# The fourth token tile of a fused SSM and SwiGLU kernel: transposed by DMA, and multiplied after six feature tiles

## The chip, the cores and the metric

The kernel runs on one core of a Trainium2 chip, in one launch. The metric is the device time in microseconds. A core has five engines with queues of their own: TensorE (PE; its weight loads are PEld), VectorE (DVE), ScalarE (ACT), GpSimd (POOL) and SyncE (SP), which here only issues DMAs. Matmul results land in PSUM, eight banks of 128 partitions by 512 fp32 values, and DVE or ACT moves them to SBUF.

## What is computed

2048 tokens of 512 features are layer-normalised; the result goes through a diagonal complex state space model (SSM) and through a SwiGLU feed-forward block, and both are added to the input:

```python
xn = layernorm(x)                                 # x: [1, 2048, 512], bf16
# SSM, 512 complex states
Lam_bar = exp(exp(log_dt) * Lambda)
B_bar = ((Lam_bar - 1) / Lambda)[:, None] * B
h[t] = Lam_bar * h[t - 1] + B_bar @ xn[t]
a = 2 * real(C @ h) + xn * Dskip
# feed-forward, 1376 hidden features
f = (silu(xn @ w_gate) * (xn @ w_up)) @ w_down
out = x + a + f
```

## The kernel before, in words

The tokens are cut into 16 tiles of 128 and four chunks of 512. The hidden features are cut into 11 feature tiles, ten of 128 and one of 96. All matmuls on normalised tokens read xnT, which holds them transposed: [128, 4 pieces k of the model width, 2048 tokens].

For a chunk, `gateup_tile` makes one feature tile: 4 matmuls (L441, one for each k) over 512 tokens into a bank for the gate, 4 into another for the up projection. `gu_out` then has ACT apply Silu to the first (L455, into guT) and copy the second (L456, into u), and for every second feature tile a product of two tiles (L460, on DVE) is put into the list `products`. `bproj_tile` (L366, evicted at L368) is the input projection of the SSM: four tiles with the real part of B, four with the imaginary part. Their weights are BT, the transposed B, which eight DMA transposes from DRAM (L140) fill. The rotations (L376 to L390, with sine and cosine tables s16 and c16), scans (L408) and rotations back of the SSM run on DVE. After that come the down projection (L575, L549) and the output of the SSM (L587), whose operand CF is made on ACT (L349) and DVE (L352).

**The first chunk** starts before all its tokens are there. Its four token tiles arrive one by one: `ln_stats` (L197, L198), the reciprocal root (L202), `norm_dve` (L214, in place in xall), then `xT_pe`: four TensorE transposes (L231) into two banks and two copies (L238, L240) into xnT. Feature tiles 0 to 2 hold six banks (`held`); `head_mm` (L676) adds the tokens that have come, 128 or 256 columns at a time. Token tile 3 is the last: `norm_dve(3)` at L713, `xT_pe(3)` at L716, and at L726 to L730 each of feature tiles 0 to 2 gets its last 128 columns and is evicted. Feature tiles 3 to 6 follow over the whole 512 columns (L785), and then the eight `bproj_tile`s of chunk 0 (L789), feature tiles 7 to 10 (L804), and `bproj_chunk(1)` (L812). The token tiles of chunks 1 to 3 are transposed by DMA: `xT_dma` (L245), which SP issues when the tile has been normalised (chunk 1 by DVE, L214; chunks 2 and 3 by ACT, L219, which needs nb of L209, which needs L205 and GpSimd's L206). The function `up_halves` (L485) is the first to read chunk 3.

**The order of the work** is the order of the program on each engine; nothing is reordered. SP's queue at the start is written out at L121 to L146: x, the weights in four groups of feature tiles (0 and 1; 2; 3 to 6; 7 to 9), x of chunk 1, four transposes of the real part of B, the last weight group, four transposes of the imaginary part, and w_last.

Work of DVE and ACT that isn't tied to a matmul (`table_ops`, the layer norm of later chunks, the SSM) stands in a backlog, each piece with a cost in us written by hand. `pump(us)` adds to a balance, and emits pieces from the backlog while the balance is at least half the cost of the next; each piece takes its cost off. `multiply(keep)` emits products until `keep` are left and takes 0.65 off for each. GU is 1.73, the cost of a feature tile; BP is 0.87. So the place of such a piece in the queue of its engine, between two evictions say, depends on how much has been pumped. `need(tag)` emits all that a tag still has.

Of the kernel before, what the change touches and what calls it, by code (L numbers as in the profile page):

```python
# [11 lines left out]
BF16 = mybir.dt.bfloat16  # L12
ALU = mybir.AluOpType
ACT = mybir.ActivationFunctionType
# [9 lines left out]
def kernel(  # L24
# [17 lines left out]
    nc = tc.nc  # L42
    _, L, D = A_x.shape
    Pst = A_Lambda_re.shape[0]
    F = B_w_gate.shape[1]
    assert L % 512 == 0 and D % 128 == 0 and Pst % 128 == 0 and Pst == D
    CW = 512
# [3 lines left out]
    TPC = CW // 128  # L51
    KD = D // 128
    NQ = Pst // 128
    FT = (F + 127) // 128
    fsz = [min(128, F - i * 128) for i in range(FT)]
# [3 lines left out]
    LA, LB = 32, 64  # L59
    FL = (FT - 1) * 128  # L60
# [6 lines left out]
    up_p = ctx.enter_context(tc.tile_pool(name="up_p", bufs=4))  # L67
# [5 lines left out]
    def bank(shape=(128, CW), dtype=F32):  # L73
        return psum.tile(list(shape), dtype, name="ps")
# [4 lines left out]
    x_v = A_x[0].rearrange("(n p) d -> p n d", p=128)  # L79
    out_v = out[0].rearrange("(n p) d -> p n d", p=128)  # L80
    wg_v = B_w_gate.rearrange("(k p) f -> p k f", p=128)
    wu_v = B_w_up.rearrange("(k p) f -> p k f", p=128)


    xall = const.tile([128, NT, D], BF16, name="xall")
    xnT = const.tile([128, KD, L], BF16, name="xnT")

    fgroups = [(0, 2), (2, 3), (3, 7), (7, FT - 1)]
    wg_g, wu_g = [], []
# [4 lines left out]
    w_last = const.tile([128, KD, 128], BF16, name="w_last")  # L94
    wu_last = const.tile([128, KD, LB], BF16, name="wu_last")
    wd_sb = const.tile([128, FT - 1, D], BF16, name="wd_sb")
    BT = const.tile([128, 2, KD, Pst], BF16, name="BT")
# [6 lines left out]
    def wslice(groups, fi, k):  # L104
        for (a, b), t in zip(fgroups, groups):
            if a <= fi < b:
                return t[:, k, (fi - a) * 128:(fi - a) * 128 + fsz[fi]]


    def load_w1(q, tiles, view, gi):  # L110
        a, b = fgroups[gi]
        q.dma_start(out=tiles[gi][:], in_=view[:, :, a * 128:min(F, b * 128)])
# [20 lines left out]
        nc.gpsimd.dma_start(out=prm_rows[i * NQ:(i + 1) * NQ, :], in_=v.rearrange("(q j) -> q j", j=128))  # L133
    load_w1(nc.sync, wg_g, wg_v, 2)
    load_w1(nc.sync, wu_g, wu_v, 2)
    for n in (TPC, TPC + 2):
        nc.sync.dma_start(out=xall[:, n:n + 2, :], in_=x_v[:, n:n + 2, :])
    for part, src in enumerate((A_B_re, A_B_im)):
        for k in range(KD):
            nc.sync.dma_start_transpose(out=BT[:, part, k, :], in_=src[:, k * 128:(k + 1) * 128])  # L140
        if part == 0:
            load_w1(nc.sync, wg_g, wg_v, 3)
            load_w1(nc.sync, wu_g, wu_v, 3)

    nc.sync.dma_start(out=w_last[:, :, 0:LB + LA], in_=wg_v[:, :, FL:F])
    nc.sync.dma_start(out=w_last[:, :, LB + LA:128], in_=wu_v[:, :, FL + LB:F])  # L146

    def load_late():
        nc.sync.dma_start(out=wu_last[:], in_=wu_v[:, :, FL:FL + LB])
# [43 lines left out]
    def xn_tile(c):  # L193
        return xn_end if c == NCH - 1 else xall[:, c * TPC:(c + 1) * TPC, :]
# [17 lines left out]
    def norm_dve(n, lo=0, hi=D):  # L212
        c, i = divmod(n, TPC)
        nc.vector.tensor_scalar(out=xn_tile(c)[:, i, lo:hi], in0=xall[:, n, lo:hi], scalar1=mv[:, n, 0:1],  # L214
                                scalar2=rstd[:, n:n + 1], op0=ALU.subtract, op1=ALU.mult)
# [8 lines left out]
    def xT_pe(n, on_dve=(), prm_too=False):  # L224

        c, i = divmod(n, TPC)
        for h in range(2):
            tp = bank((128, HK * 128 + 128), BF16)
            for k in range(HK):
                lo = (h * HK + k) * 128  # L230
                nc.tensor.transpose(out=tp[:, k * 128:(k + 1) * 128], in_=xn_tile(c)[:, i, lo:lo + 128],  # L231
                                    identity=ident[:])
            if prm_too and h == 1:
                prm_transpose(tp[:, HK * 128:])
            dst = xnT[:, h * HK:(h + 1) * HK, n * 128:(n + 1) * 128]
            src = tp[:, 0:HK * 128].rearrange("p (k t) -> p k t", k=HK)
            if h in on_dve:
                nc.vector.tensor_copy(out=dst, in_=src)  # L238
            else:
                nc.scalar.copy(out=dst, in_=src)  # L240
        return tp[:, HK * 128:]

    def xT_dma(n):
        c, i = divmod(n, TPC)
        nc.sync.dma_start_transpose(out=xnT[:, :, n * 128:(n + 1) * 128], in_=xn_tile(c)[:, i, :])  # L245
# [12 lines left out]
    V = nc.vector  # L258

    def prm_transpose(pp):  # L260
        nc.tensor.transpose(out=pp, in_=prm_rows[:], identity=ident[:])
# [173 lines left out]
    u_pair = {}  # L435
    products = []

    def gu_mm(ps, groups, c, fi, lo, hi):
        fs = fsz[fi]
        for k in range(KD):  # L440
            nc.tensor.matmul(ps[:fs, lo:hi], lhsT=wslice(groups, fi, k),  # L441
                             rhs=xnT[:, k, c * CW + lo:c * CW + hi], start=(k == 0), stop=(k == KD - 1))

    def gu_tile(c):
        if c not in gu_tiles:
            gu_tiles[c] = gut.tile([128, FT - 1, CW], BF16, name="guT")
        return gu_tiles[c]

    def gu_out(c, fi, psg, psu):

        guT = gu_tile(c)
        fs = fsz[fi]
        if fi % 2 == 0:
            u_pair[c] = up_p.tile([128, 2, CW], BF16, name="u2")
        nc.scalar.activation(out=guT[:fs, fi, :], in_=psg[:fs], func=ACT.Silu)  # L455
        nc.scalar.copy(out=u_pair[c][:fs, fi % 2, :], in_=psu[:fs])  # L456
        if fi % 2 == 1:
            lo = fi - fi % 2
            g, u = guT[:fs, lo:fi + 1, :], u_pair[c][:fs, 0:fi - lo + 1, :]
            products.append(lambda: V.tensor_tensor(out=g, in0=g, in1=u, op=ALU.mult))  # L460

    up_last = {}

# [40 lines left out]
    def gateup_tile(c, fi):  # L504
        if fi == FT - 1:
            return gateup_last(c)
        psg = bank()
        gu_mm(psg, wg_g, c, fi, 0, CW)
        psu = bank()
        gu_mm(psu, wu_g, c, fi, 0, CW)  # L510
        gu_out(c, fi, psg, psu)
# [97 lines left out]
    def queue(tag, ops, at=None):  # L609
        ops = [[op[0], op[1], op[2] if len(op) > 2 else None, tag] for op in ops]  # L610
        if at is None:
            backlog.extend(ops)
        else:
            backlog[at:at] = ops

    def step():
        for item in backlog[0:AHEAD + 1]:
            if item[2] is not None:
                item[2]()
                item[2] = None  # L620
        cost, op, _, _ = backlog.pop(0)
        op()
        owed[0] -= cost

    def pump(us):

        owed[0] += us
        while backlog and owed[0] >= backlog[0][0] * 0.5:
            step()
        if not backlog:  # L630
            owed[0] = 0.0

    def multiply(keep):

        while len(products) > keep:
            products.pop(0)()
            owed[0] -= 0.65
# [7 lines left out]
    GU = 8 * 0.2163  # L645
    BP = 4 * 0.2163
    H = 3
    held = [(bank(), bank()) for _ in range(H)]
# [23 lines left out]
    def head_mm(which, lo, hi, ks, fis):  # L672

        for fi in fis:
            for k in ks:
                nc.tensor.matmul(held[fi][which][:, lo * 128:hi * 128], lhsT=wslice((wg_g, wu_g)[which], fi, k),  # L676
                                 rhs=xnT[:, k, lo * 128:hi * 128], start=(k == 0), stop=(k == KD - 1))

    allk = range(KD)
# [31 lines left out]
    params_a(pp)  # L711
    head_mm(1, 0, 2, allk, (2,))
    norm_dve(3)  # L713
    head_mm(0, 2, 3, range(0, HK), range(H))
    head_mm(1, 2, 3, range(0, HK), range(H))
    xT_pe(3, on_dve=(0, 1))  # L716
    head_mm(0, 2, 3, range(HK, KD), range(H))
    head_mm(1, 2, 3, range(HK, KD), range(H))
    tables = table_ops()
# [3 lines left out]
    queue("tables", tables[2:3])  # L723
    queue("ln1", norm1)
    queue("tables", tables[3:4] + [(0.1, params_sin)] + tables[4:])
    for fi in range(H):  # L726
        head_mm(0, 3, 4, allk, (fi,))
        head_mm(1, 3, 4, allk, (fi,))
        gu_out(0, fi, *held[fi])
        pump(GU / 4)  # L730
    pump(2.0)

    def bproj_chunk(c):
        need(f"ln{c}")
# [47 lines left out]
        queue(f"ssm{c}", fwd + back)  # L782

    G0 = 7
    for fi in range(H, G0):  # L785
        gateup_tile(0, fi)
        pump(GU)
        multiply(1)
# [72 lines left out]
```

## Time and profile before

| what | value |
|---|---|
| median of 3 runs | 178.78 us (178.36 to 178.89) |
| the profiled execution | 178.79 us |
| its span, first to last instruction | 177.0 us |
| granted TensorE clock | 1.000 |
| busy: PE, DVE, ACT, POOL | 173.4, 154.0, 94.2, 51.3 us |
| matmuls at L441 over 512 columns | 296 |
| DMA transposes on SP: L140, L245 | 8 of 1.18 to 1.36 us, 12 of 1.19 to 1.25 us |
| their time from issue to landing, min/median/max | 3.0/4.5/6.5 us at L140, 2.4/2.4/3.1 us at L245 |

The timeline gives start and length of instructions in us from the span's start, merged where neighbours are alike; what stands in brackets is the idle time of the engine before the instruction and what ended it. SPq is SP's queue: its rows are the issues of DMAs, not the transfers. The DMA view has the time from issue to landing. A matmul row that stands alone shows its whole latency, so costs of TensorE are read from the starts of neighbours, or from the pieces of the chain of work that ended last, which don't overlap.

### The profile page before, as it was taken

What the parts mean: (1) busy time and instruction counts of PE and PEld (TensorE: products, weight loads), DVE (VectorE), ACT (ScalarE), POOL (GpSimd) and SP (SyncE); (2) the same over time, 40 slices, a digit from 0 to 9 for tenths busy, and PEclk for the clock granted to TensorE, in tenths of its full rate; (3) what the DMA queues carried; (4) which work ended last, traced back from release to release, by engine and by line L of the source; (5) the groups of instructions that cost most, each with busy time, mean ns of one, the idle gap of its engine ahead of it and who ended that gap; (6) DMA issues with size and microseconds to landing.
All of it is one profiled execution on the core that took longest, in us unless ns stands there. A gap on an engine that the chain in (4) does not pass through costs nothing.

```text
span 177.0 us, 2543 instructions
## 1 busy us (share of the span) xinstructions
PE 173.4 (98%) x927; PEld 82.3 (46%) x927; DVE 154.0 (87%) x234; ACT 94.2 (53%) x167; POOL 51.3 (29%) x85
## 2 busy tenths in 40 slices
PE   8999999999999999999999999999999999999993
PEld 2984444444444444444444444444444444444443
DVE  3789997999999996899999999999999999993033
ACT  3468898967299649923766661053866610001300
POOL 6050300000300050003999640058185250001410
PEclk9999999999999999999999999999999999999999
DMA  5998745996141016900000020019659600000662
GB/s 169 279 297 215 141 88 122 361 206 111 22 88 31 4 28 117 348 11 2 20 17 19 15 67 24 4 17 132 88 78 178 116 9 0 0 0 6 63 99 74
DMA packets 30764, 16.23 MB, mean 92 GB/s; under 512 B 19680, under 2 KB 30560, under 8 KB 30720
## 3 DMA queue, kind: packets, MB, share of 16 engines
q1 hardware_dynamic: 24704, 11.44, 27.9%
q0 software_dynamic: 5184, 4.07, 16.0%
q10 hardware_dynamic: 864, 0.56, 1.0%
q8 instruction: 7, 0.11, 0.3%
q14 instruction: 5, 0.04, 0.1%
HBM read 8.33 MB, written 5.24 MB: 77 GB/s over the span
## 4 chain that ended last, share of the span: by engine, by line
PE 96%; DMA 1%; DVE 1%; issue 0%
PE ps L441 36%; PE ps L587 16%; PE ps L366 16%; PE ps L575 10%; PE ps L549 10%; PE ps L676 3%; PE ps L496 2%; PE ps L538 2%; DMA xall<-in_A_x_dram 1%; PE ps L485 1%; PE ps L231 1%; DVE stats L197 0%; PE ps L653 0%; DVE xall L214 0%; DVE stats L684 0%; DVE res L592 0%
## 5 line engine op out<-in xcount | busy, mean ns | idle before, releaser
L441 PE MATMUL ps<-xnT,wu 128*128 128x512 bf16 x148 | 38.0, 379 | 0.0
L441 PE MATMUL ps<-xnT,wg 128*128 128x512 bf16 x148 | 38.0, 379 | 0.0
L408 DVE TENSOR_TENSOR_SCAN g<-r_t,car,u 128x512 bf16<-128x512 f32 x24 | 28.7, 1260 | 0.0
L455 ACT ACTIVATE guT<-ps 128x512 bf16<-128x512 f32 x40 | 24.4, 611 | 7.3 <-PE ps L441 5.5
L366 PE MATMUL ps<-xnT,BT 128*128 128x512 bf16 x128 | 28.3, 379 | 0.0
L587 PE MATMUL ps<-CF,wt 128*128 128x512 bf16 (+2 forms) x144 | 28.2, 356 | 0.0
L456 ACT CAST u<-ps 128x512 bf16<-128x512 f32 x40 | 23.9, 598 | 5.6 <-PE ps L441 5.6
L600 ACT CAST res<-ps 128x512 bf16<-128x512 f32 x12 | 6.7, 590 | 36.0 <-PE ps L587 26.8
L181 POOL DMA_DIRECT2D gu_rows<-ul x36 | 17.6, 498 | 18.1 <-DVE ul L473 18.1
L441 PEld LDWEIGHTS <-wu 128*128 128x128 bf16 x148 | 14.5, 98 | 17.4
L441 PEld LDWEIGHTS <-wg 128*128 128x128 bf16 x148 | 14.4, 98 | 17.2
L368 ACT CAST u<-ps 128x512 bf16<-128x512 f32 x32 | 18.4, 591 | 5.1 <-PE ps L366 4.9
L601 POOL DMA_DIRECT2D out_dram<-res x12 | 10.6, 1224 | 34.3 <-ACT res L600 34.2
L587 PEld LDWEIGHTS <-wt 128*128 128x128 bf16 x144 | 13.3, 98 | 15.0 <-issue 0.8
L366 PEld LDWEIGHTS <-BT 128*128 128x128 bf16 x128 | 12.5, 98 | 15.1
L206 POOL TENSOR_TENSOR rstd<-ve,neg_half 128x4 f32<-128x4 f32 x3 | 5.2, 1730 | 47.0 <-DVE ve L205 47.0
L575 PE MATMUL ps<-wd_sb,guT 128*128 128x512 bf16 x80 | 17.6, 379 | 0.0
L549 PE MATMUL ps<-wd_sb,guT 128*128 128x512 bf16 x80 | 17.4, 379 | 0.0
L460 DVE TENSOR_TENSOR guT<-guT,u 128x1024 bf16<-128x1024 bf16 x20 | 13.5, 678 | 0.0
L575 PEld LDWEIGHTS <-guT 128*128 128x128 bf16 x80 | 7.8, 98 | 9.4
L549 PEld LDWEIGHTS <-guT 128*128 128x128 bf16 x80 | 7.8, 98 | 9.5
L197 DVE BATCH_NORM_STATS2 stats<-xall 128x6 f32<-128x512 bf16 x14 | 9.5, 677 | 1.9 <-DMA xall<-in_A_x_dram 1.9
(114 smaller groups left out, 194.7 us busy)
## 6 DMA issues: line engine op xcount, KB each, us to landing
out_dram<-in_A_x_dram SPq DMA_DIRECT2D x1, 1536.0 KB, 7.1
out_dram<-res POOLq DMA_DIRECT2D x12, 128.0 KB, 3.5
out_dram<-xall POOLq DMA_DIRECT2D x3, 512.0 KB, 7.6
wd_sb<-in_B_w_down_dram SPq DMA_DIRECT2D x2, 640.0 KB, 9.0
xall<-in_A_x_dram SPq DMA_DIRECT2D x1, 1024.0 KB, 7.2
gu_rows<-ul POOLq DMA_DIRECT2D x36, 8.0 KB, 1.6
wg<-in_B_w_gate_dram SPq DMA_DIRECT2D x1, 512.0 KB, 5.0
wu<-in_B_w_up_dram SPq DMA_DIRECT2D x1, 512.0 KB, 6.1
```

What stands on the lines that cost most here:

```text
L181: nc.gpsimd.dma_start(out=gu_rows[c][i * RT:(i + 1) * RT, p, :], in_=product[p * RT:(p + 1) * RT, i * 128:(i + 1) * 128])
L366: nc.tensor.matmul(ps[:], lhsT=BT[:, part, k, q * 128:(q + 1) * 128], rhs=xnT[:, k, c * CW:(c + 1) * CW], start=(k == 0), stop=(k == KD - 1))
L368: nc.scalar.copy(out=u_tiles[c][:, part, q, :], in_=ps[:])
L408: V.tensor_tensor_scan(out=g()[:, part, q, :], data0=r_t[:, q:q + 1].to_broadcast([128, CW]), data1=u_tiles[c][:, part, q, :], initial=ini ...
L441: nc.tensor.matmul(ps[:fs, lo:hi], lhsT=wslice(groups, fi, k), rhs=xnT[:, k, c * CW + lo:c * CW + hi], start=(k == 0), stop=(k == KD - 1))
L455: nc.scalar.activation(out=guT[:fs, fi, :], in_=psg[:fs], func=ACT.Silu)
L456: nc.scalar.copy(out=u_pair[c][:fs, fi % 2, :], in_=psu[:fs])
L460: products.append(lambda: V.tensor_tensor(out=g, in0=g, in1=u, op=ALU.mult))
L549: nc.tensor.matmul(o[:], lhsT=gu_tiles[k][:, fi, i * 128:(i + 1) * 128], rhs=wd_sb[:, fi, :], start=(fi == 0), stop=False)
L575: nc.tensor.matmul(o[:], lhsT=gu_tiles[c][:, fi, i * 128:(i + 1) * 128], rhs=wd_sb[:, fi, lo:hi], start=(fi == 0), stop=False)
L587: nc.tensor.matmul(o, lhsT=w_tiles[c][:, part, q, i * 128:(i + 1) * 128], rhs=CF[:, part, q, lo:hi], start=(fresh and part == 0 and q == 0 ...
L601: nc.gpsimd.dma_start(out=out_v[:, n, :], in_=res[:], accum_op=ALU.add)
```

## The change

Token tile 3 of chunk 0 is no longer transposed by TensorE. After `norm_dve(3)`, SP issues `xT_dma(3)`, and the loads that stood behind chunk 1's x in SP's queue now follow it, in a function `load_mid`: both parts of B first, then the last weight group and w_last. The two loads of chunk 1's x become one.

Feature tiles 0 to 2 are evicted over the first 384 columns (EC) as soon as token tile 2 is in. Feature tiles 3 to 5 are then made over the same 384 columns, first the three gates, then the three ups. Token tile 3 comes after that, for six feature tiles: `end_mm` puts 128 columns of four gates into one bank and of four ups into another, then two gates and two ups into a third; `end_out` evicts them, four tiles' gates at once and two tiles' ups at once. The products of pairs 0 and 1, 2 and 3, 4 and 5 are listed only then. The pumps have other sizes. From feature tile 6 on the program is as before. The lines ahead are those of the kernel before.

```diff
     load_w1(nc.sync, wu_g, wu_v, 2)
-    for n in (TPC, TPC + 2):
-        nc.sync.dma_start(out=xall[:, n:n + 2, :], in_=x_v[:, n:n + 2, :])
-    for part, src in enumerate((A_B_re, A_B_im)):
-        for k in range(KD):
-            nc.sync.dma_start_transpose(out=BT[:, part, k, :], in_=src[:, k * 128:(k + 1) * 128])
-        if part == 0:
-            load_w1(nc.sync, wg_g, wg_v, 3)
-            load_w1(nc.sync, wu_g, wu_v, 3)
-
-    nc.sync.dma_start(out=w_last[:, :, 0:LB + LA], in_=wg_v[:, :, FL:F])
-    nc.sync.dma_start(out=w_last[:, :, LB + LA:128], in_=wu_v[:, :, FL + LB:F])
+    nc.sync.dma_start(out=xall[:, TPC:2 * TPC, :], in_=x_v[:, TPC:2 * TPC, :])
+
+    def load_mid():
+        for part, src in enumerate((A_B_re, A_B_im)):
+            for k in range(KD):
+                nc.sync.dma_start_transpose(out=BT[:, part, k, :], in_=src[:, k * 128:(k + 1) * 128])
+        load_w1(nc.sync, wg_g, wg_v, 3)
+        load_w1(nc.sync, wu_g, wu_v, 3)
+        nc.sync.dma_start(out=w_last[:, :, 0:LB + LA], in_=wg_v[:, :, FL:F])
+        nc.sync.dma_start(out=w_last[:, :, LB + LA:128], in_=wu_v[:, :, FL + LB:F])
...
-    def gu_out(c, fi, psg, psu):
...
+    def product(c, fi):
+        g, u = gu_tile(c)[:, fi - 1:fi + 1, :], u_tile(c, fi)[:]
+        products.append(lambda: V.tensor_tensor(out=g, in0=g, in1=u, op=ALU.mult))
+
+    def gu_out(c, fi, psg, psu, hi=CW):
+
+        nc.scalar.activation(out=gu_tile(c)[:, fi, 0:hi], in_=psg[:, 0:hi], func=ACT.Silu)
+        nc.scalar.copy(out=u_tile(c, fi)[:, fi % 2, 0:hi], in_=psu[:, 0:hi])
+        if fi % 2 == 1 and hi == CW:
+            product(c, fi)
...
     norm_dve(3)
+    xT_dma(3)
+    load_mid()
     head_mm(0, 2, 3, range(0, HK), range(H))
     head_mm(1, 2, 3, range(0, HK), range(H))
-    xT_pe(3, on_dve=(0, 1))
     head_mm(0, 2, 3, range(HK, KD), range(H))
     head_mm(1, 2, 3, range(HK, KD), range(H))
...
+    EARLY = 2 * H
+    EC = (TPC - 1) * 128
     for fi in range(H):
-        head_mm(0, 3, 4, allk, (fi,))
-        head_mm(1, 3, 4, allk, (fi,))
-        gu_out(0, fi, *held[fi])
-        pump(GU / 4)
-    pump(2.0)
+        gu_out(0, fi, *held[fi], hi=EC)
+    psg = [bank() for fi in range(H, EARLY)]
+    for fi in range(H, EARLY):
+        gu_mm(psg[fi - H], wg_g, 0, fi, 0, EC)
+        pump(GU * 3 / 8)
+    for fi in range(H, EARLY):
+        psu = bank()
+        gu_mm(psu, wu_g, 0, fi, 0, EC)
+        gu_out(0, fi, psg[fi - H], psu, hi=EC)
+        pump(GU * 3 / 8)
+
+    def end_mm(ps, at, groups, fi):
+        for k in range(KD):
+            nc.tensor.matmul(ps[:, at * 128:(at + 1) * 128], lhsT=wslice(groups, fi, k), rhs=xnT[:, k, EC:CW],
+                             start=(k == 0), stop=(k == KD - 1))
+
+    def end_out(fis, psg, psu):
+        guT = gu_tile(0)
+        nc.scalar.activation(out=guT[:, fis[0]:fis[-1] + 1, EC:CW],
+                             in_=psg.rearrange("p (f t) -> p f t", t=128), func=ACT.Silu)
+        for i in range(0, len(fis), 2):
+            nc.scalar.copy(out=u_tile(0, fis[i])[:, :, EC:CW],
+                           in_=psu[:, i * 128:(i + 2) * 128].rearrange("p (f t) -> p f t", t=128))
+            product(0, fis[i + 1])
+
+    psg, psu = bank(), bank()
+    for ps, groups in ((psg, wg_g), (psu, wu_g)):
+        for fi in range(4):
+            end_mm(ps, fi, groups, fi)
+    end_out(range(4), psg[:], psu[:])
+    pump(GU)
+    multiply(1)
+    ps = bank()
+    for i, groups in enumerate((wg_g, wu_g)):
+        for fi in range(4, EARLY):
+            end_mm(ps, 2 * i + fi - 4, groups, fi)
+    end_out(range(4, EARLY), ps[:, 0:256], ps[:, 256:512])
+    pump(GU / 2)
+    multiply(1)
...
-    for fi in range(H, G0):
+    for fi in range(EARLY, G0):
         gateup_tile(0, fi)
```

More of the change, by code (lines that the diff above doesn't have):

```diff
@@ L447, in gu_tile, with u_tile @@
         return gu_tiles[c]
-    def gu_out(c, fi, psg, psu):
[L451 to L460, printed above, removed]
+    def u_tile(c, fi):
+        if (c, fi // 2) not in u_pair:
+            u_pair[c, fi // 2] = up_p.tile([128, 2, CW], BF16, name="u2")
+        return u_pair[c, fi // 2]
+    def product(c, fi):
[6 more added lines that the diff above has]
+            product(c, fi)
     up_last = {}
```

## The prediction

> **What bounds it now.** I read the chain of work that ended last first, because it says which engine to price: 96% of the span is TensorE, and its pieces join without a hole through the head.
>
> ```profile
> 9.86 0.22 PE ps L231 x4
> 10.09 2.01 PE ps L676 x36
> 12.10 6.91 PE ps L441 x32
> 19.00 6.91 PE ps L366 x32
> 25.91 5.18 PE ps L441 x24
> ```
>
> The reader is to see that each piece starts where the last ended, and the unit prices: 0.22/4 = 55 ns for a transpose, 2.01/36 = 55.8 ns for a matmul over 128 columns with its own weight load, 6.91/32 = 215.9 ns for one over 512. So the kernel can gain only what leaves TensorE, and it loses every wait that TensorE is given; nothing later gives it back, since the chain is TensorE to the end.
>
> Next I read the timeline of SP, whose queue the change reorders.
>
> ```profile
> 7.03 5.37 SPq L140 DMA_TRANSPOSE BT<-in_A_B_re_dram  x4
> 12.45 0.58 SPq L112 DMA_DIRECT2D wg<-in_B_w_gate_dram  x1
> 13.08 1.14 SPq L112 DMA_DIRECT2D wu<-in_B_w_up_dram  x1
> 14.26 5.09 SPq L140 DMA_TRANSPOSE BT<-in_A_B_im_dram  x4
> 19.41 0.58 SPq L145 DMA_DIRECT2D w_last<-in_B_w_gate_dram  x1
> 20.03 0.51 SPq L146 DMA_DIRECT2D w_last<-in_B_w_up_dram  x1
> 22.03 5.16 SPq L245 DMA_TRANSPOSE xnT<-xall  x4
> ```
>
> SP issues one thing after another and a transpose holds it 1.3 us. Last, DVE, ACT and TensorE where the change shifts their order: three places where one waits for another.
>
> ```profile
> 9.11 0.40 DVE L214 TENSOR_SCALAR xall<-xall,mv,rstd 128x512 bf16<-128x512 bf16 x1
> ...
> 30.34 1.23 DVE L376 TENSOR_TENSOR pm<-u,c 128x2048 bf16<-128x2048 bf16 x1 [1.12 <-ACT c L305]
> ...
> 61.78 0.16 DVE L205 TENSOR_SCALAR ve<-mv 128x4 f32<-128x4 f32 x1
> 61.90 1.22 DVE L386 TENSOR_TENSOR wt<-pm 128x2048 bf16<-128x2048 bf16 x1
> 63.04 0.68 DVE L460 TENSOR_TENSOR guT<-guT,u 128x1024 bf16<-128x1024 bf16 x1
> 64.03 0.16 DVE L209 SCALAR_TENSOR_TENSOR nb<-mv,rstd 128x4 f32<-128x4 f32 x1 [0.30 <-POOL rstd L206]
> ```
>
> ```profile
> 64.22 0.81 ACT L219 ACTIVATE xn_end<-xall,nb,rstd 128x512 bf16<-128x512 bf16 x1 [3.16 <-DVE nb L209]
> ```
>
> ```profile
> 72.46 1.92 PE L485 MATMUL ps<-xnT,wu_last 128*64 128x512 bf16 x16
> ```
>
> The reader is to see that DVE at 30.34 waits for a sine on ACT, and that the transposed chunk 3, which L485 reads, hangs on DVE's L209 through ACT's L219.
>
> **TensorE's own work.** Four transposes go: 4 x 55 = 0.220 us. The 24 matmuls of feature tiles 3 to 5 over 512 columns become 24 over 384 and 24 over 128; tile 3 of features 0 to 2 keeps its 24. A 384-wide one isn't in the trace; on the line between 55.8 and 215.9 ns it is 162.5, so a pair costs 2.4 ns more, 0.06 us for 24 (bounds: nothing, and 24 x 55.8 = 1.34 us if a pair cost a whole extra narrow one; the rows lie on the line, so I take 0.06). Net: **-0.16 us**. The 0.06 comes from 128-wide matmuls at 55.8 ns each. The Trainium skill (TensorE: Matmul & The Clock Gate, Back-to-back issue gap) speaks against the split: it gives about 81 ns for a 128-wide and 131 ns for a 512-wide matmul when weight loads alternate with matmuls, by which, as an estimate on its line, each split would cost 64 ns and the net would be +1.2 us. The trace disagrees, 36 such in 2.01 us, so this gets no part of the sum.
>
> **Token tile 3 by DMA.** Its normalisation (L214) ends at 9.52 and moves by nothing: everything ahead of it on DVE and TensorE stays. In 22.03's row the issue follows its normalisation by 0.03, so SP issues at 9.55. Landing is 2.4 us after issue where SP's queue is otherwise idle (median of L245), and 5.9 for the first L140 of 7.03, which stood behind 1.5 MB of loads; so 11.95 to 15.4. That row itself landed at 12.9 and only needed those loads drained, so I take 12.9. It is read after feature tiles 3 to 5: tile 2 ends at 10.76 - 0.22 = 10.54, then 24 x 162.5 ns = 3.90, so 14.44. Hidden by 1.5 us. The weights of feature tile 3 are now read at 10.54 and not 11.9; they landed at 4.26 + 5.0 = 9.3, the up half at 10.9 against 12.5.
>
> **The moved loads.** SP now has nothing from 6.0 to 9.55, and all of L140, the last weight group and w_last stand behind the wait for that normalisation. Issues: 9.55 tile 3, then spacing 1.30 (5.16 for four at L245, its first gap 1.32): B_re from 10.87 to 14.77, B_im from 16.07 to 19.97 (before: 14.26 to 18.10). B_re lands 3.0 later, 17.8, and is read from 18.7: hidden. The last B_im landed 3.0 after issue, the last row of L140; its neighbours of C_im took 2.6 to 3.8. So it lands at 22.97 (22.6 to 23.9). L366 starts at 18.84 and the matmul with the fourth k of B_im is its 20th: 18.84 + 19 x 0.2159 - 0.16 = 22.78, its weight load 0.1 earlier. TensorE waits about **0.3 us** (0 to 1.2), where before it had 1.6 to spare. (L366 began before B_im had landed, so a matmul doesn't wait for all of BT; if it waits for a whole part, it is 0.9 us.) Gate group 3 is issued at 21.3 and read at 25.7: with 4.6 us to landing, as at 12.45, it would be 0.2 late, but then B_re stood in front with 1.35 us between their landings, so 24.4. Chunk 1's four transposes end SP's line by 29.4 + 2.4 = 31.8 at worst, 30.6 with short issues; they are read at 31.6. In SP's file that has a us or none; I take none.
>
> The price of the transposes that decides here is SP's 1.3 us. The Trainium skill (DMA: Bandwidth & Descriptors, Latency and other measured facts) gives DMA transposes 261 GB/s, an estimated 0.5 us for 128 KB; by that B_im would have landed by 18 and the 0.3 us were nothing. The rows have 1.30 between issues with the DMA engines half idle (share 0.46 from 18.84 to 25.75), so the row goes into the sum.
>
> **ACT and banks.** 5 more instructions, and the first six evictions start near 10.1 instead of 11.02. Back to back they are 0.48 us apart at 512 columns, 0.37 at 384; TensorE fills a bank each 0.65. Two banks are free at 10.54 (tile 2's, copied by 9.2), the third is held[0]'s, read by 10.6. No wait; nothing, unless ACT lags by more than the 1.2 us until the third is wanted.
>
> **The ledger of queued work.** This is the second place that can cost. Up to feature tile 6 the pumps were 3 x 0.43 + 2.0 + 3 x 1.73 = 8.49 us, less two products at 0.65; now 6 x 0.65 + 1.73 + 0.87 = 6.49, less the same. All queued work is 2.0 us of cost later in the program, about one feature tile. DVE is in time at first (two copies of 0.28 gone), its second half c ends at 29.3 as before. But the sine behind it is now emitted after feature tile 8, not 7: that copy starts at 29.24, the sine 0.5 later, so L376 starts at 30.84, **0.5 late**, and DVE has no hole until L205. Two products of chunk 1 (0.6 each) are now ahead of L205: 61.78 + 0.5 + 1.2 = 63.5. L205 to L209 takes 2.25 (61.78 to 64.03), to ACT 0.19: 65.9. In the rows the four L219 reach from 64.22 to 68.06; now one more copy (0.47) stands among them, so the last starts at 70.2, ends at 71.0, lands by 73.5. L485 reads chunk 3 from its ninth matmul on, 72.46 + 9 x 0.116 - 0.16 = 73.3. TensorE waits **0.2 us** (0 to 0.9), where it had 2.0 to spare. Chunk 2's, by the same steps, land at 56.3 and are read at 56.7.
>
> **Sum.** -0.16 + 0.3 + 0.2 = +0.34 us on the profiled execution's 178.79 (span 177.0 and 1.8 around it), which is the median of the runs, 178.78. I predict **179.1 us**. A measurement of this kernel can tell about 0.3%, 0.54 us, from no change.
>
> **The rivals.**
> A, all hidden: B_im lands 2.6 after issue and chunk 3 in time: -0.16, 178.6. For it: C_im's shortest landing. Against: SP's four extra us ahead of L140.
> B, slower: SP's queue is what decides. From the point where the fourth B_im lands after 22.7, each further us is a us. With 3.8 to landing (C_im's longest) and 1.36 between issues (B_re's, 5.37 for four) it lands at 24.2: 1.5 us of wait, 180.3. For it: loads may still share the DMA engines; against: those are drained by then.
> C, slower: the ledger is dearer than I price it, and chunk 3 or the CF operands behind it are 0.8 us late: with 0.3 for B_im, 179.7.
> D, tile 3's transpose lands at 15.4 (5.9 after issue) and the change only moves the wait: 1.0 us in place of 0.22: 180.1 with the rest.
> E, faster by more than 0.54: TensorE would have to hold idle time that its rows don't show.
>
> **How the numbers follow.** Forecast (both waits small, -0.1 to +0.54) 0.43, A 0.10, B 0.27, C 0.12, D 0.05, E 0.03. Within 0.3%: 0.43 + 0.10 = 0.53; slower: 0.44; faster: 0.03. The range reaches from A (178.5) past B (180.5).
>
> **What would show it.** In the profile after: SP's L245 at 9.55 ahead of both L140; no L231 at 9.8; 24 pairs at L441 in 3.9 us. Right: a hole of TensorE near 22.7 waiting for a DMA into BT, and one near 73.4 at L485; L376 starts near 30.8. Wrong: no hole at 22.7 (then SP or landing is faster than the rows), a hole near 14.4 (D), or one where I have none, such as at 25.7 or 31.6.

## The result and the profile after

The changed kernel takes 180.02 us (median of 6 runs, 179.76 to 180.4) against 178.51 for the kernel before on the same chip (6 runs, 178.36 to 178.89): 1.5 us more, ratio 1.0082 with a 95% interval of 1.0067 to 1.0098. The profiled execution took 179.76 us with a span of 178.0 (before: 178.79 and 177.0). Line numbers from here on are those of the changed kernel: the transposes of B are L141, token tiles L244, gate and up L440, the late matmuls of token tile 3 L745, bproj L365, wu_last's L487, the matmuls with CF L589. Where an experiment shifts them, its lines carry its own numbers; tile and shape tell which is which.

The page's chain of work, by engine, was 96% TensorE. It is now:

```profile
PE 89%; DMA 4%; DVE 3%; ACT 1%; issue 0%; DVEq 0%
```

The pieces of that chain in order of time, as start, length, what. They answer to the five pieces shown of before.

```profile
10.18 3.90 PE ps L440 x24
14.08 2.82 PE ps L745 x48
16.90 1.73 PE ps L440 x8
...
27.88 4.49 DMA xnT<-xall
32.37 0.14 issue
32.50 7.07 PE ps L365 x32
```

The reader is to see two things. The 24 matmuls over 384 columns take 3.90 us, as worked out. And the chain leaves TensorE for a transfer that the prediction priced at nothing: the fourth transpose of chunk 1's tokens, issued at 27.88 and landed at 32.37. Between 22.10 and 27.88, in the part left out, the page puts work of ACT and DVE (evictions, sine and cosine) ahead of that issue. It isn't what the transpose waited for: DVE had normalised chunk 1 by 23.24, and SP was busy issuing from 9.19 to 29.75. TensorE's own timeline gives all holes; a hole is the next start less the last start and the matmuls between (0.216 us each over 512 columns).

```profile
11.97 2.11 PE L440 MATMUL ps<-xnT,wu 128*128 128x384 bf16 x12
14.05 1.07 PE L745 MATMUL ps<-xnT,wg 128*128 128x128 bf16 x16
...
18.47 7.25 PE L365 MATMUL ps<-xnT,BT 128*128 128x512 bf16 x32
25.55 1.03 PE L440 MATMUL ps<-xnT,wg 128*128 128x512 bf16 x4
26.71 1.04 PE L440 MATMUL ps<-xnT,wu 128*128 128x512 bf16 x4
...
31.04 1.03 PE L498 MATMUL ps<-xnT,w_last 128*128 128x512 bf16 x4
32.50 7.07 PE L365 MATMUL ps<-xnT,BT 128*128 128x512 bf16 x32 [0.44 <-DMA xnT<-xall]
```

Token tile 3: 14.05 - 11.97 - 12 x 0.1625 = 0.13. B's fourth imaginary piece: 25.55 - 18.47 - 6.91 = 0.17. Up weights of group 3: 26.71 - 25.55 - 0.86 = 0.30. Chunk 1: 32.50 - 31.04 - 0.86 = 0.60. At L487 (73.24 to 75.17, 16 matmuls that take 1.85 without a hole) 0.08. Sum 1.28, less 0.16 of TensorE's own work: +1.12. The weight loads' waits name the same culprits (line, what it waited for, us in total, times, longest):

```profile
PEld L440 <- DMA wu<-in_B_w_up_dram: 0.6, 1, 0.6
PEld L365 <- DMA BT<-in_A_B_im_dram: 0.5, 1, 0.5
...
PEld L745 <- DMA xnT<-xall: 0.4, 1, 0.4
```

**Closing the account.** The first matmul with CF starts at 75.10 (before: 74.31), +0.79. The head of this execution ran 0.36 us faster, before anything that the change touches: tile 2's part ends at 10.18, where before's rows less four transposes give 10.54. So 1.12 - 0.36 = 0.76 of the 0.79 is accounted for; 0.2 more arise behind 161, where the last matmuls begin 0.78 later but the span ends 1.0 later. The execution profiled of before stood 0.3 above the median of the runs made beside it, so the two profiles' difference (0.97) is less than the medians' (1.5).

SP's timeline, for the rows of before:

```profile
5.37 0.90 SPq L136 DMA_DIRECT2D xall<-in_A_x_dram  x1
9.19 1.31 SPq L244 DMA_TRANSPOSE xnT<-xall  x1
10.55 5.52 SPq L141 DMA_TRANSPOSE BT<-in_A_B_re_dram  x4
16.11 5.17 SPq L141 DMA_TRANSPOSE BT<-in_A_B_im_dram  x4
21.33 0.58 SPq L112 DMA_DIRECT2D wg<-in_B_w_gate_dram  x1
...
23.66 6.09 SPq L244 DMA_TRANSPOSE xnT<-xall  x4
```

Tile 3 and the first of B's real part are issued 0.3 to 0.4 earlier than predicted, with the head. B's real part then takes 5.52 and not 5.2, and from the imaginary part on the issues are within 0.05 of where the prediction put them. What differs is the last row: chunk 1's four transposes now follow straight behind four loads. Their time to landing, min, median and max, was 2.4/2.4/2.5 in the profile before. After:

```profile
L244 SPq DMA_TRANSPOSE xnT<-xall x4: 1211/1361/1875, 23.7 to 27.9; - x4
...
DMA to landing us min/median/max: 4.1/4.7/5.1
```

DVE and ACT, for the rows of before:

```profile
31.28 1.23 DVE L375 TENSOR_TENSOR pm<-u,c 128x2048 bf16<-128x2048 bf16 x1 [2.39 <-ACT c L304]
...
64.06 0.17 DVE L204 TENSOR_SCALAR ve<-mv 128x4 f32<-128x4 f32 x1
64.13 1.22 DVE L385 TENSOR_TENSOR wt<-pm 128x2048 bf16<-128x2048 bf16 x1
66.28 0.16 DVE L208 SCALAR_TENSOR_TENSOR nb<-mv,rstd 128x4 f32<-128x4 f32 x1 [0.93 <-POOL rstd L205]
```

```profile
66.48 0.81 ACT L218 ACTIVATE xn_end<-xall,nb,rstd 128x512 bf16<-128x512 bf16 x1 [2.98 <-DVE nb L208]
```

DVE waits for the sine until 31.28 (30.34 before). Chunk 3's variance starts at 64.06 (61.78), its nb at 66.28 (64.03) and its first normalisation at 66.48 (64.22): 2.3 us later. SP ends the issue of its four transposes at 72.80 (70.22), 2.6 later, while TensorE is 0.8 later. That uses up nearly all of the 2.0 us it had to spare.

### The profile page after: what moved, and what is told of

The parts are those of the page before. It is cut to its first block, busy times and chain, and to the rows that moved or that the text cites. A ratio compares the mean times of both kernels' runs of the same rounds, so it can differ in the third digit from the quotient of the medians.

```text
span 178.0 us, 2588 instructions
## 1 busy us (share of the span) xinstructions
PE 173.0 (97%) x947; PEld 82.5 (46%) x947; DVE 153.5 (86%) x232; ACT 95.5 (54%) x172; POOL 51.3 (29%) x85
## 4 chain that ended last, share of the span: by engine, by line
PE 89%; DMA 4%; DVE 3%; ACT 1%; issue 0%; DVEq 0%
PE ps L440 32%; PE ps L589 16%; PE ps L365 14%; PE ps L551 10%; PE ps L577 10%; DMA xnT<-xall 3%; PE ps L678 2%; PE ps L745 2%; PE ps L540 2%; PE ps L498 1%; DMA xall<-in_A_x_dram 1%; PE ps L487 1%; DVE pm L300 1%; DVE pm L299 1%; ACT u L367 1%; ACT s L304 1%
## 5 line engine op out<-in xcount | busy, mean ns | idle before, releaser
L440 PE MATMUL ps<-xnT,wu 128*128 128x512 bf16 (+1 forms) x148 | 37.0, 375 | 0.1
L440 PE MATMUL ps<-xnT,wg 128*128 128x512 bf16 (+1 forms) x148 | 37.0, 375 | 0.0
L365 PE MATMUL ps<-xnT,BT 128*128 128x512 bf16 x128 | 28.5, 379 | 0.4 <-DMA xnT<-xall 0.4
L589 PE MATMUL ps<-CF,wt 128*128 128x512 bf16 (+2 forms) x144 | 28.2, 356 | 0.0
L459 ACT ACTIVATE guT<-ps 128x512 bf16<-128x512 f32 (+1 forms) x40 | 23.7, 593 | 5.9 <-PE ps L440 5.7
L460 ACT CAST u<-ps 128x512 bf16<-128x512 f32 (+1 forms) x40 | 23.1, 577 | 6.6 <-PE ps L440 6.6
L367 ACT CAST u<-ps 128x512 bf16<-128x512 f32 x32 | 18.5, 586 | 7.2 <-PE ps L365 7.2
L440 PEld LDWEIGHTS <-wu 128*128 128x128 bf16 x148 | 14.4, 98 | 17.2 <-DMA wu<-in_B_w_up_dram 0.6
L440 PEld LDWEIGHTS <-wg 128*128 128x128 bf16 x148 | 14.4, 98 | 16.4 <-DMA wg<-in_B_w_gate_dram 0.2
L589 PEld LDWEIGHTS <-wt 128*128 128x128 bf16 x144 | 13.2, 98 | 15.1 <-issue 0.8
L365 PEld LDWEIGHTS <-BT 128*128 128x128 bf16 x128 | 12.4, 98 | 16.0 <-issue 0.9
L455 DVE TENSOR_TENSOR guT<-guT,u 128x1024 bf16<-128x1024 bf16 x20 | 13.4, 679 | 0.0
L375 DVE TENSOR_TENSOR pm<-u,c 128x2048 bf16<-128x2048 bf16 x8 | 9.8, 1220 | 2.5 <-ACT c L304 2.4
```

What stands on the lines that cost most here:

```text
L365: nc.tensor.matmul(ps[:], lhsT=BT[:, part, k, q * 128:(q + 1) * 128], rhs=xnT[:, k, c * CW:(c + 1) * CW], start=(k == 0), stop=(k == KD - 1))
L367: nc.scalar.copy(out=u_tiles[c][:, part, q, :], in_=ps[:])
L459: nc.scalar.activation(out=gu_tile(c)[:, fi, 0:hi], in_=psg[:, 0:hi], func=ACT.Silu)
L460: nc.scalar.copy(out=u_tile(c, fi)[:, fi % 2, 0:hi], in_=psu[:, 0:hi])
L589: nc.tensor.matmul(o, lhsT=w_tiles[c][:, part, q, i * 128:(i + 1) * 128], rhs=CF[:, part, q, lo:hi], start=(fresh and part == 0 and q == 0 ...
```

## The experiments

Theories. **Q**: the loss is TensorE waiting for what SP's new order brings late. **L**: it is the 2.0 us of pumps that are missing up to feature tile 6. **M**: the split matmuls and the extra evictions cost by themselves. **Q2**, formed on the way: transposes land late because loads share the DMA engines with them. The kernel before lay at 178.4 to 178.5 beside all of them.

**The order of the matmuls alone.** TensorE transposes tile 3, SP's loads are those of before; splits, evictions and pumps are the changed ones.

```diff
-    xT_dma(3)
-    load_mid()
...
+    xT_pe(3, on_dve=(0, 1))
```

> The order of the matmuls and evictions of the changed kernel, with its pumps, but token tile 3 transposed by TensorE and SP's loads in the order of before. Theory Q (the loss is waits that SP's new order makes: 0.14 us for tile 3, 0.17 for B_im, 0.30 for the up weights of group 3, 0.60 for chunk 1's transposed tokens in the changed kernel's profile): those holes are gone, left is 0.06 for the narrower matmuls, so 178.6. Theory L (the ledger, work emitted 2 us of cost later, makes the loss): most of the 1.5 us stays, 179.3 to 180. Theory M (a 384- and a 128-wide matmul cost much more than one of 512): 24 x 64 ns, 180.0.

Measured 179.16, ratio 1.0038 (1.0026 to 1.0050). TensorE has one new hole, at the tenth matmul that reads wu_last, where L said:

```profile
72.19 1.27 PE L488 MATMUL ps<-xnT,wu_last 128*64 128x512 bf16 x9
73.75 1.02 PE L488 MATMUL ps<-xnT,wu_last 128*64 128x512 bf16 x7 [0.29 <-DMA xnT<-xn_end]
```

Nine take 1.04, so 0.52 is lost. Q alone had said 178.6: L is real, 0.5 us where nothing else is late.

**The same with the pump given back.**

```diff
     end_out(range(4, EARLY), ps[:, 0:256], ps[:, 256:512])
-    pump(GU / 2)
+    pump(GU / 2 + 2.0)
     multiply(1)
```

> e1 (order of the matmuls alone, tile 3 by TensorE, SP's loads as before) with 2.0 more pumped behind the last eviction of token tile 3. e1 took 179.16 with one hole of 0.5 us on TensorE, at the first matmul on chunk 3. Theory L for that part (work emitted 2 us of cost late makes chunk 3 late): the hole goes, 0.06 for the narrower matmuls is left, 178.5 to 178.6. Rival (the 0.69 of e1 is the price of the narrower matmuls, or of the five more instructions on ACT): 179.1 as in e1.

Measured 178.58, ratio 1.0010 (1.0000 to 1.0020), no hole. 24 matmuls over 384 columns again take 3.90 us. So M, which asks for 1.5 us, is refuted: order, split and evictions together cost 0.1 us (by the interval 0 to 0.4).

**The changed kernel with the pump given back**, the same edit on the changed kernel.

> The changed kernel with 2.0 more pumped behind the last eviction of token tile 3, so that the queued work stands from feature tile 6 on about where it stood before. Theory Q: SP's order is the same, so the four holes up to 32.5 stay and only the 0.08 near 73 goes: 179.9. Theory L: 178.5 to 179.0, and the hole at chunk 1 goes because its tokens are normalised earlier.

Measured 179.81, ratio 1.0076 (1.0064 to 1.0088). By the medians L's share of the loss is 0.2 us and not 0.5, but the intervals overlap, and a second set of runs of the changed kernel, below, has 180.3. The traces say more: L's hole at L487, only 0.08 in the changed kernel, goes (16 in 1.85). Of Q's holes two stay:

```profile
23.10 2.98 PE L365 MATMUL ps<-xnT,BT 128*128 128x512 bf16 x13 [0.50 <-DMA BT<-in_A_B_im_dram]
25.92 1.03 PE L440 MATMUL ps<-xnT,wg 128*128 128x512 bf16 x4
27.07 1.04 PE L440 MATMUL ps<-xnT,wu 128*128 128x512 bf16 x4
```

Here B is 0.66 late and the up weights 0.29, together 0.95 against 1.20 without L487 in the changed kernel; tile 3 and chunk 1 are in time. TensorE, waiting more early, comes to chunk 1 0.36 us later. But chunk 1's last transpose also landed 2.7 us after its issue at 28.2, and not 4.5, with the same four loads ahead of it in SP's queue. In the kernel of the next experiment, which has that order too, it took 2.5. The rows of all four transposes of chunk 1, first in this kernel and then in that one:

```profile
L244 SPq DMA_TRANSPOSE xnT<-xall x4: 1211/1236/1507, 24.0 to 28.2; - x4
DMA to landing us min/median/max: 2.7/3.3/4.1
```

```profile
L244 SPq DMA_TRANSPOSE xnT<-xall x4: 1216/1216/1533, 23.7 to 28.0; - x4
DMA to landing us min/median/max: 2.5/2.8/4.0
```

So the loads ahead don't by themselves make chunk 1 land as late as in the changed kernel, where all four had landed by 27.4, ahead of the last transpose's issue at 27.88. What did is not shown.

**The DMA part alone.** SP's new order, with the matmuls in the order of before, which read token tile 3 straight away.

```diff
     norm_dve(3)
+    xT_dma(3)
+    load_mid()
...
-    xT_pe(3, on_dve=(0, 1))
```

> The other half alone: tile 3 by DMA and SP's loads behind it, as in the changed kernel, but matmuls, evictions and pumps in the order of before, so tile 3 is wanted right after token tile 2, near 10.2 us. Theory Q: tile 3 lands near 14.0 as in the changed kernel, TensorE waits 3.5 to 3.8 us there, and being late then waits for none of the other loads: 178.5 - 0.2 + 3.6 = 181.9, with the holes at B_im, at the up weights and at chunk 1 gone. If tile 3 landed in its undisturbed 2.4 us (11.6), the wait were 1.4 and the time 179.7.

Measured 184.63, ratio 1.0304 (1.0261 to 1.0347). I had expected 181.9, with a wait of 3.6 us for tile 3. In the profiled execution (184.57) it was 4.5, since tile 3 landed 5.5 us after its issue:

```profile
PE ps L675 <- DMA xnT<-xall: 4.5, 1, 4.5
```

So making feature tiles 3 to 5 first does what it is for: it covers all but 0.13 of such a wait. The miss has a second part. Behind the wait TensorE's granted clock was 0.50 from 14.7 to 17.3, where 24 matmuls over 128 columns took 2.51 us instead of 1.34, and 0.79 from there to 18.4, where four over 512 took 1.10 instead of 0.86. The page gives the granted clock in 40 slices of the span, in tenths of full speed; the 6 among the nines is the slice from 13.7 to 18.3:

```profile
PEclk9996999999999999999999999999999999999999
```

That is 1.4 us. The six executions follow the granted clock: 182.34 at 1.000, 183.25 and 184.57 at 0.991, 184.69 to 185.20 at 0.981. The one at full clock is within 0.5 us of what was expected.

**The weights off SP's queue.** In `load_mid`, group 3 and w_last are issued by POOL, between 11.3 and 14.4, while SP issues transposes.

```diff
-        load_w1(nc.sync, wg_g, wg_v, 3)
-        load_w1(nc.sync, wu_g, wu_v, 3)
+        load_w1(nc.gpsimd, wg_g, wg_v, 3)
+        load_w1(nc.gpsimd, wu_g, wu_v, 3)
```

(w_last's two lines likewise.)

> The changed kernel with the last weight group and w_last issued by POOL behind its parameter arithmetic (it is done near 11.4 us) and not by SP behind B_im. Theory Q: the weights are in before B_im, chunk 1's transposes start as soon as they are normalised with no loads in front, so the hole for the up weights (0.30) and that for chunk 1 (0.60) go and tile 3's and B_im's (0.31) stay: 180.0 - 0.9 = 179.1. Theory L: no change, 180.0. If plain loads in flight slow the B transposes, the hole at B_im grows: 179.5 or more.

Measured 180.72, ratio 1.0117 (1.0100 to 1.0135): slower, where 179.1 was expected. SP issues B's real part as before, but it lands late, in this kernel

```profile
L141 SPq DMA_TRANSPOSE BT<-in_A_B_re_dram x4: 1259/1270/1592, 10.5 to 14.7; - x4
...
DMA to landing us min/median/max: 4.5/6.3/7.0
```

against 2.6/3.0/4.1 in the changed one, and TensorE loses 1.7 us to it by its starts, 1.4 by its waits. That is Q2: bytes in flight beside B's transposes made them late, though SP issued them as before. The Trainium skill (DMA: Bandwidth & Descriptors, Issuing engines are not separate DMA queues) says that DMAs of all issuing engines run on the same 16 DMA engines and interleave; these landings agree. The holes for the up weights and for chunk 1 are gone. Chunk 1's first two transposes land in 2.5 and 2.4 us again; the last two took 4.3 and 3.3 with none of those loads left in flight, which Q2 doesn't explain. And L's hole is there in full, 0.60, though TensorE was 1.7 us late:

```profile
75.23 1.02 PE L487 MATMUL ps<-xnT,wu_last 128*64 128x512 bf16 x7 [0.37 <-DMA xnT<-xn_end]
```

**Two of B's transposes ahead.** They are issued in SP's gap behind chunk 1's x, ahead of tile 3; the pump is given back.

```diff
+    for i in range(2):
+        load_B(i)
...
-        for part, src in enumerate((A_B_re, A_B_im)):
+        for i in range(2, 2 * KD):
+            load_B(i)
```

> The changed kernel with 2.0 more pumped, and with two of the eight B transposes issued in the time in which SP waits for tile 3 (behind chunk 1's x). Theory Q1 (it is the length of SP's queue behind tile 3 that makes the holes): all that follows is issued 2.6 us earlier, the holes at B_im, at the up weights and at chunk 1 go; but tile 3 now stands behind two transposes that land 5.9 us after issue as in the kernel before, so near 15, 1.0 late: 178.5 - 0.2 + 1.0 = 179.3. Rival Q2 (the holes come from loads that slow the transposes beside them, wherever they stand): 179.8 as in e4, with more at tile 3.

Measured 180.59, ratio 1.0135 (1.0106 to 1.0165). Every hole from 16 us on is gone; one is left:

```profile
15.48 1.07 PE L751 MATMUL ps<-xnT,wg 128*128 128x128 bf16 x16 [1.39 <-DMA xnT<-xall]
```

Two transposes behind the loads held SP 3.71 us, so tile 3 was issued at 9.96 instead of 9.19, and landed 5.5 us later. What B gained, tile 3 lost.

**Three ahead, x behind tile 3**, with and without the pump.

```diff
-    nc.sync.dma_start(out=xall[:, TPC:2 * TPC, :], in_=x_v[:, TPC:2 * TPC, :])
+    for i in range(3):
+        load_B(i)
...
     def load_mid():
+        nc.sync.dma_start(out=xall[:, TPC:2 * TPC, :], in_=x_v[:, TPC:2 * TPC, :])
```

> The changed kernel with 2.0 more pumped, three of the B transposes issued while SP waits for tile 3, and chunk 1's x (512 KB) issued behind tile 3. Theory Q1: tile 3 has no 512 KB load in front and lands by 12.5; everything behind it is issued 3 to 4 us earlier; no hole is left, x is in by 15, 0.5 to 1 later than DVE wants it, which delays only DVE: 178.5 - 0.16 = 178.3 to 178.5, level with the kernel before or a little under it. Rival Q2: transposes and loads mixed land later whatever the order, 179 or more. If DVE's delay reaches chunk 3, 178.8.

> e7 without the 2.0 that it pumps more, so SP's order mended and the ledger as in the changed kernel. Theory L: with SP's holes gone, the hole at the first matmul on chunk 3 comes out in full, 0.5 us as in e1, so e7 + 0.5: 178.8 to 179.0. If the ledger costs nothing by itself, it is level with e7.

Measured 180.14, ratio 1.0094 (1.0080 to 1.0109), and without the pump 180.55, 1.0114 (1.0101 to 1.0128). The step of 0.4 is what L says, but the intervals overlap; the level missed by 1.7. In the first kernel tile 3 is still 0.45 late; and x came late for DVE, which waited 1.70 us. DVE doesn't make it up by 49, and ACT, which normalises chunk 2 in program order ahead of evictions, held TensorE's banks back:

```profile
49.30 0.81 ACT L224 ACTIVATE xall<-xall,nb,rstd 128x512 bf16<-128x512 bf16 x1 [5.15 <-DVE nb L214]
```

```profile
50.65 1.02 PE L446 MATMUL ps<-xnT,wg 128*128 128x512 bf16 x4 [0.43 <-ACT guT L465]
```

The second kernel's trace has none of these holes. It has 0.67 at chunk 2's tokens and L's, 0.49 at L493, so the step between the two isn't L's hole alone:

```profile
57.43 7.07 PE L371 MATMUL ps<-xnT,BT 128*128 128x512 bf16 x31 [0.50 <-DMA xnT<-xall]
...
74.59 1.02 PE L493 MATMUL ps<-xnT,wu_last 128*64 128x512 bf16 x7 [0.27 <-DMA xnT<-xn_end]
```

**A seventh feature tile over 384 columns**, as more cover for tile 3, with one or two of B's transposes ahead and the pump given back.

```diff
+    more = [(bank(), bank()) for fi in range(EARLY, 7)]
+    for (psg6, psu6), fi in zip(more, range(EARLY, 7)):
+        gu_mm(psg6, wg_g, 0, fi, 0, EC)
+        gu_mm(psu6, wu_g, 0, fi, 0, EC)
...
     for fi in range(EARLY, G0):
-        gateup_tile(0, fi)
+        end_mm(more[fi - EARLY][0], 3, wg_g, fi)
+        end_mm(more[fi - EARLY][1], 3, wu_g, fi)
+        gu_out(0, fi, *more[fi - EARLY])
```

> The changed kernel with 2.0 more pumped, one of the B transposes issued while SP waits for tile 3, and the first 384 columns of feature tile 6, too, ahead of token tile 3, which is then wanted 1.3 us later, near 15.3. Theory Q1: tile 3, behind one transpose, lands by 15; all behind it is issued 1.3 us earlier, B_im lands by 21.5 against 22.6, the weights and chunk 1 in time: no hole, 178.5 - 0.16 = 178.3. Rival Q2 (loads in flight slow whatever transposes stand behind them): chunk 1's still land 4 to 5 us after issue and B_im is late by some tenths: 178.8 to 179.2.

> As e9 with two B transposes issued while SP waits for tile 3, as in e6, whose one hole was 1.4 us at tile 3. Theory Q1: the 1.3 us of matmuls put ahead of it fill that hole, 0.1 is left: 178.4 to 178.6. Rival Q2: tile 3 is later still, 179.

Measured 180.22, ratio 1.0100 (1.0086 to 1.0113), and 180.07, ratio 1.0086 (1.0073 to 1.0099). With one ahead there is no hole up to 49 us: every wait of Q is gone. The loss is elsewhere, in the first kernel on DVE and then on TensorE:

```profile
17.59 0.69 DVE L461 TENSOR_TENSOR guT<-guT,u 128x1024 bf16<-128x1024 bf16 x1 [1.06 <-ACT u L764]
```

```profile
51.93 1.02 PE L446 MATMUL ps<-xnT,wg 128*128 128x512 bf16 x4 [0.70 <-ACT guT L465]
```

The products come only when tile 3 is in; with one more tile ahead of it DVE runs dry for 1.06 us at 17, is a us late at chunk 2's normalisation, and TensorE loses about 1.1 us at 49 to 57. The second loses 0.8 at 49 to 53, and besides 0.13 at tile 3 and 0.52 at chunk 2's tokens. The profiled execution of the first took 179.53 and its median 180.22; what the other executions lost beyond that no trace shows.

**The changed kernel once more**, with no edit.

> The changed kernel once more, for a second profile of it: 180.0. If the holes are the loss, their sum in this profile follows its time: 1.29 us of holes stood in the execution of 179.76, so one of 180.2 has some 1.7. Which hole grows tells which landing varies.

Measured 180.3, ratio 1.0103 (1.0082 to 1.0124); its profiled execution took 180.03. Tile 3 has no hole this time, B 0.54, the up weights 0.15, chunk 1 0.87, L487 none: 1.56 against 1.28, and 0.27 us more of time. The same program has the same sum within 0.3, split otherwise.

**x behind tile 3, no transpose moved**: the edit of x of three ahead, without `load_B`; the pump is given back.

> The changed kernel with the 2.0 us of pump given back, and the load of chunk 1's tokens issued behind token tile 3's transpose instead of ahead of it; no transpose is moved. It asks why token tile 3 lands 4.2 to 5.6 us after its issue in every run so far. Theory Q2 (a transpose that shares the DMA engines with a load in flight lands late): with the load behind it, token tile 3 is issued near 9.2 and lands in 2.4 to 3.2 us, by 12.4, and TensorE has no hole there. Rival (a lone transpose of this size in this place takes this long whatever lies beside it): it lands in 4.2 to 4.8 us as before, and the hole of 0.0 to 0.5 us at 13.9 stays. The price in both: the tokens were landed 4.8 us after issue when they were issued behind in the run with three transposes ahead; issued at 10.5 they land near 15.3, VectorE wants them near 14.1 and waits about 1.2 us, and, as in that run, its delay comes out as 0.5 to 1 us of holes near 50 in which TensorE lacks a bank. The wait for the fourth imaginary piece of B stays near 0.4. Time by that 179.4 to 180.2; under 179.0 would say that VectorE's delay is free here.

Measured 180.55, ratio 1.0125 (1.0100 to 1.0149). Tile 3 landed 3.4 us after its issue, between the two theories' numbers and under every run with x ahead (4.2 to 5.6); with x behind but three of B's transposes ahead it had been 4.6 and 4.3. So what is issued just ahead explains part of its lateness; its issue took SP 2.34 instead of 1.31, so some of the delay only moved into the queue. DVE waited for x as expected:

```profile
15.29 0.69 DVE L196 BATCH_NORM_STATS2 stats<-xall 128x6 f32<-128x512 bf16 x1 [1.26 <-DMA xall<-in_A_x_dram]
```

I had expected 0.4 for B's imaginary part and 0.5 to 1 us of bank holes near 50. There was no hole near 50. TensorE had by then lost 1.5 us to B, issued 1.1 us later:

```profile
22.66 0.39 PE L365 MATMUL ps<-xnT,BT 128*128 128x512 bf16 x1 [0.31 <-DMA BT<-in_A_B_im_dram]
23.93 2.98 PE L365 MATMUL ps<-xnT,BT 128*128 128x512 bf16 x13 [0.88 <-DMA BT<-in_A_B_im_dram]
```

No version beat the kernel before; the nearest, 178.58, is the one that leaves its loads alone.

## Why the prediction was right or wrong

The direction was forecast, and that TensorE would wait for what SP's new order brings. Of the five holes two had a price; the other three were named as what could show me wrong, and priced at nothing. +0.34 was predicted, +1.5 measured. The likeliest case, within 0.3%, did not come; rival B's mechanism did (SP's queue decides), with the price spread over three places. That B's 180.3 is near the measured 180.02 is luck in its parts: B's path has the last transpose of the imaginary part land at 24.2, and it landed at 22.7.

- **TensorE, -0.16: right.** 24 narrower pairs in 3.90 us and 48 over 128 columns in 2.68 (in the kernel with the order alone, where no hole is among them), both as the rows had it. The net of +1.2 that the prediction worked out from the Trainium skill's figures (24 x 64 - 220 ns is 1.3) doesn't come: order and ledger without the DMA part end 0.1 from before.
- **Tile 3, "hidden by 1.5 us": the size was wrong.** It was issued 0.36 earlier than 9.55, with the head, and landed at 14.0 instead of 12.9: 4.8 after issue. The step "that row itself landed at 12.9 and only needed those loads drained" failed: the load ahead was now x in one piece, which itself landed 8.0 after issue, at 13.4. Cost 0.13 (0.0 in the second profile). Making tiles 3 to 5 first covered the rest.
- **B's imaginary part, +0.3: right** in place and size (0.17 and 0.54 in two profiles, 2.7 to landing, 1.29 between issues). Two small errors cancel in it: it landed 0.3 earlier than I said, and TensorE came 0.37 earlier. The Trainium skill's 261 GB/s (DMA: Bandwidth & Descriptors, Latency and other measured facts), by which there would be no hole, doesn't hold for these: 128 KB each 1.29 us is about 100 GB/s.
- **Group 3, "so 24.4": failed.** The gate landed 4.0 after its issue, at 25.3, and cost nothing; the up half, issued 0.63 behind it, took 4.7 and came 0.30 late. I worked out the gate and let it stand for both; by my own 4.6 us the up half had 26.5 against 26.6.
- **Chunk 1, "a us or none; I take none": the largest term.** 0.60 and 0.87. The step that failed is 2.4 us to landing, read in a profile where two small loads stood well ahead of these transposes. Behind group 3 and w_last, the order that the change makes, they took 4.1 to 5.1 and, in the second profile, 4.0 to 5.3; the first and last issues held SP 1.5 and 1.9 us instead of 1.2. I had named the bound and took the end that no row of such an order supported. (The 31.8 adds the 2.4 to the end of SP's issue; the profile counts it from the start, which gives some 30.5, so the landing alone made it late.) Why the last ones took so long stays open: with the same loads ahead they took 2.5 and 2.7 in two other kernels.
- **The ledger, +0.2: its sum right, its parts not.** Alone it costs 0.5. Here it is 0.08 at L487 in one profile and nothing in the other; the medians' 0.2 (180.02 against 179.81) isn't clear of the noise. L375 starts at 31.28, 30.8 was said, since ACT comes later too.
- **ACT and banks at nothing: right** for the changed kernel; the runs with x later or seven tiles show where that cover ends.

What is shown: with SP's order of before, the new order of the matmuls and the pump cost 0.1 us; with SP's new order and the same pump, 1.3. What stays open: why a transpose holds SP 1.5 to 2.3 us in some places and 1.2 in others; how the landing of a transpose divides between what is ahead in the queue, bytes beside it, and what neither explains; and the 0.2 us behind 161.

## What to carry to other kernels

A duration from issue to landing belongs to the order it was read in: when a change puts transfers behind other transfers, take the landing from a row with the same neighbours, or the longer bound, and price every transfer behind the moved ones, up to the last consumer. Where one engine is busy from end to end and its transfers come just in time, moving a transfer earlier may only pick another one to be late: the versions here with the new order of matmuls and SP's loads changed moved 1.3 to 2.3 us of loss between tile 3, B, the weights, chunks 1 to 3 and DVE's queue. Read each hole's price against the lateness already there: a late engine can hide the next wait, as at L487 in the changed kernel, but needn't, as with the weights on POOL.

## What the runs showed of the hardware

- Chunk 1's four transposes by DMA landed 2.4 to 2.5 us after issue in the profile before, where SP's last load ahead was issued 2.0 us earlier. Straight behind four plain loads they took 4.1 to 5.1 and 4.0 to 5.3 in two profiles of the changed kernel, but 2.7 to 4.1 and 2.5 to 4.0 in two other kernels with the same loads ahead.
- Loads issued by POOL beside the transposes of B's real part moved their landing from 2.6 to 4.1 us to 4.5 to 7.0, while SP's issues stayed the same.
- SP held most transposes 1.2 to 1.3 us, but single ones longer: 1.31 for tile 3 behind the load of x and 2.34 without it, 3.71 for two of B's behind that load.
- A load of 512 KB for x landed 8.0 us after its issue behind the weights' loads, 3.8 us behind one transpose.
- After a wait of 4.5 us TensorE's granted clock was 0.50 for 2.6 us, which cost 1.4 us with what followed; five of that kernel's six executions had a mean granted clock of 0.981 to 0.991. In the profiled executions with waits of 1.4 us and less it stayed at 0.998 to 1.000.
- The first matmuls ran slow for a varying time: eight over 128 columns took 0.97 us in the profile before and 0.72 after, and the head differed by 0.36 us with the same work.
